# A Trainium2 attention and MLP kernel: a written-out program order in place of a planner, one pool of eight PSUM banks, and one head pair more on the half-array path

## The chip, the cores and the metric

The kernel runs on one core of one Trainium2 chip. The metric is the device time of one execution in microseconds (us), lower is better. Runs of the kernel before took 312.3, 311.33 and 309.93 us; the median is 311.33 us. Engines are named as in the profile: PE is the matrix engine, DVE the vector engine, ACT the scalar engine, POOL the general engine that here issues the loads, and SP the engine that issues the other DMAs.

## What is computed

Block-sparse attention over 4 batches of 8 heads, 768 positions and 64 dimensions, followed by an MLP over tokens and then over channels. Cut to what matters:

```python
scores = q @ k.T / sqrt(64)                        # per batch and head, 768 x 768
mask = window of +-1 block | first and last block row and column | 3 sampled blocks per block row
attn = softmax(where(mask, scores, -1e9))          # blocks are 32 x 32
x = (attn @ v), heads side by side                 # (4, 768, 512)
a1 = alpha1 * x + beta1
u = x + lam * (w_tok @ a1)                         # w_tok is 768 x 768
ch = relu((alpha2 * u + beta2) @ w_ch1) @ w_ch2    # 512 -> 2048 -> 512
out = u + lam * ch
```

## The kernel before

**Units of work.** The 32 heads are handled as 16 pairs (four pairs per batch). The transposed scores of a pair are cut into nine units of 1024 columns, each two PSUM banks, so there are 144 units. Per unit there is one exponential on ACT (PSUM to SBUF, f16) and the products with the values on PE. After the ninth unit the two accumulators are normalised on DVE (L701, L704) into `x_sb`.

**Two ways to make scores.** The first `NPE = 6` pairs (0 to 5) are *single* (`single`, L714): the scores of one head at a time, with a contraction of 88 rows. 64 of them are the head's dimensions and 24 are rows of the block mask, so the mask costs no separate step (matmuls L729, exponentials L744, values L769). Their transposed queries and keys come from transposes on PE (L641, helper L294) and copies out of PSUM (L363). The other ten pairs are *paired* (`paired`, L791): both heads of a pair are computed at once on two halves of the array, 64 rows each (`qk_group`, matmuls L850, in groups of two or three units). There is no room for mask rows there. After the exponential (L802) DVE takes the minimum with a tile `maskT` that holds zeros where the mask is off (L807). Their queries and keys are transposed by DMA transposes that SP issues (`xt`, L668 to L673), two for each pair, from a staging tile `rel` of which there are three.

**The mask tile.** DVE makes 24 rows (`mrow`, L550), SP writes them to DRAM (`mout`, L557), and SP reads them back in 18 transfers that spread each row over the partitions of `maskT` (`min_`, L561 to L572). The planner releases this step by `MASK_AT = 28`.

**The MLP.** Per batch: scale and shift on DVE (L942, L950), the token product on PE (L962, in groups of 18 matmuls), the residual add (L972), the second scale (L978), a transpose (by SP's DMA at L1010, or on PE at L1000). Then comes the channel MLP in half batches of 384 tokens: 16 first products (L1044, four matmuls each), each followed by a relu on ACT (L1057) or on DVE (L1061), then second products (L1106), a residual add on DVE (L1123) and a store that SP issues (L1130).

**Loads.** POOL issues them in a fixed order (`LOADS`, L43, then the later pairs). From pair 8 on (p > NPE + 1) each waits for a flag that DVE writes (L417), which POOL reads with a one-element copy (L397).

**What sets the order.** The kernel's source holds a planner. Every step is a `Job` (L340) with an engine, a cost, a priority and its dependencies; an event loop (L1233 to L1363) plays the engines against time and issues the job with the lowest priority key that can go. It also decides by simulated free times which bank a step takes and, for steps that can run on either, whether ACT or DVE does them. Where PE would be idle in the plan, `fill` (L254) issues matmuls on zeros (L252). `pin_order` (L67) then fixes the instruction order of each engine, and `bank_order` (L84) orders the users of each bank.

**PSUM.** Six banks are in one tile `ps6`, a seventh is `ps7`, and an eighth carries the tag `ops`. Score units take pairs of banks (b0+b1, b2+b3, b4+b5); single pairs take only the last two of these (`PAIRS[1:]`, L752).

Of the kernel before, what the change touches and what calls it, by code (L numbers as in the profile page):

```python
# [11 lines left out]
FP = mybir.dt.float32  # L12
# [20 lines left out]
NPAIR = H // 2  # L33
VW = D + 2
UN = 1024
NU = 9
NS = NPAIR * NU
NPE = 6
NET = 11
LEADS = (18, 18, 18, 18, 18, 18, 18, 18, 19, 18, 18, 18, 18, 18, 18, 18)  # L40
PATS = (800.0, 800.0, 800.0, 800.0, 1200.0, 800.0, 0.0, 800.0, 800.0, 400.0, 800.0, 800.0, 800.0, 800.0, 800.0, 800.0)
NUDGE = {}
LOADS = (  # L43
    "v 0", "q 1", "k 1", "v 1", "q 2", "k 2", "tok 0", "tok 1", "tok 2", "v 2", "lam", "a1",
    "b1", "q 3", "v 3", "k 3", "a2", "be2", "q 4", "k 4", "v 4", "w1 0", "w1 1", "w1 2",
    "w1 3", "q 5", "k 5", "v 5", "q 6", "k 6", "v 6",
)
PR = 1
EARLY = ('b0', 'b1')
OLD = True  # L50
MROW = (2, 3, 9)
W2AT = (0, 1, 2, 7.5)
NSPLIT = 0
UTN = 0
TOKP = 1
COVER = 800.0
NLD = 6
HOLD = 2
T0 = 6600.0
MASK_AT = 28  # L60
AHEAD = 13000.0
SCALE = 1.0 / 8.0
EXPB = -0.35667494
F16MAX = 65504.0

# [71 lines left out]
def kernel(  # L137
# [78 lines left out]
    ps6 = ps.tile([P, 6 * 512], FP, name="ps6", tag="ps6", bufs=1)  # L216
    ps7 = ps.tile([P, 512], FP, name="ps7", tag="ps7", bufs=1)
    ps6_name = [ps6[:].tensor.name]
    BANKS = tuple(f"b{i}" for i in range(6))
    ALL = BANKS + ("b6",)  # L220
    PAIRS = ("b0+b1", "b2+b3", "b4+b5")

    def bank(name, shape, dt=FP):
        t = ps7[:, :] if name == "b6" else ps6[:, ts(ALL.index(name), 512)]
        if dt != FP:
            t = t.bitcast(dt)
        t = t[:, 0 : int(np.prod(shape[1:]))]
        return t if len(shape) == 2 else t.rearrange("p (o c) -> p o c", o=shape[1])

    def two_banks(names):  # L230
        return ps6[:, ts(PAIRS.index(names), UN)]

# [17 lines left out]
    def keep_warm(n, w, name="b6"):  # L250
        for _ in range(n):
            nc.tensor.matmul(bank(name, [P, w]), warm[:, 0:P], warm[:, 0:w], start=True, stop=True)  # L252

    def fill(ns):  # L254
        free = [x for x in ("b6", "b0", "b1") if slots[x] > 0]
        while ns > 60.0 and free:
            w = min(512, int(ns * 2.4))
            keep_warm(1, w, free[0])
            ns -= w / 2.4 + 3.0

    keep_warm(7, 512)
    keep_warm(2, P)
# [17 lines left out]
    rel0 = wk.tile([P, 2, NT, 2 * D], BF, name="rel", tag="rel", bufs=3)  # L280

    def first_cast(a):
        for i, src in enumerate((q2f, k2f)):
            sl = src[:, a, :].rearrange("p (o d) -> p o d", o=NT)
            dst = rel0[:, a, :, i * D : (i + 1) * D]
            if a == 0 and i == 1:
                nc.scalar.copy(out=dst, in_=sl)
            else:
                nc.vector.tensor_copy(out=dst, in_=sl)

    def transposes(rel, a, name, slots=range(NT)):
        tps = bank(name, [P, NT, P], BF)
        for o in slots:
            nc.tensor.transpose(tps[:, o, :], rel[:, a, o, :], identb[:])  # L294
        return tps.rearrange("p o c -> p (o c)")
# [3 lines left out]
    flatA = transposes(rel0, 0, "b0", range(0, 3))  # L299
    flatB = transposes(rel0, 0, "b1", range(3, 6))  # L300
    bqs = []
    for w in range(2):
        t = ps.tile([P, 512], FP, name="ops", tag="ops", bufs=1) if w else bank("b2", [P, 512])
# [15 lines left out]
    keep_warm(7, P)  # L319
    for j in range(2, NQB):  # L320
# [4 lines left out]

    ACT_COPY = dict(ACT=790.0)
    dma_free = [8000.0]
    SEM = 70.0  # L330
    DRAIN = 166.0
    free_at = dict(NEVER=1e9, NONE=0.0, PE=T0, ACT=T0, DVE=T0, POOL=4800.0, SP=T0)
    slots = dict(
        **{b: 1 for b in ALL}, ops=1, eT=NET, head=NQB, vext=NV, ld=NLD, rel=3,
        x=NXB, uT=3, hts=2, a1p=2, ub=2, ot=2, w2b=1,
    )
    jobs = []
    now = [0.0]

    class Job:  # L340
        def __init__(self, eng, dur, prio, fn, deps=(), take=(), give=(), lat=None):
            self.eng = eng if isinstance(eng, tuple) else (eng,)
            self.dur, self.prio, self.fn = dur, prio, fn
            self.deps = list(deps)
            self.take, self.give = take, give
            self.lat = lat
            self.alt = {}
            self.xfer = None
            self.late = 0.0
            self.moves = False  # L350
            self.done = None
            self.gate = None
            self.marks = []
            self.n = len(jobs)
            if prio in NUDGE:
                self.prio = (prio[0] + NUDGE[prio],) + prio[1:]
            jobs.append(self)

    def copy(eng, out, in_):
        if eng == "ACT":  # L360
# [4 lines left out]
    def Copy(prio, fn, deps, take=(), give=(), only=False):  # L365
        j = Job(("DVE", "NEVER") if only else ("ACT", "DVE"), 550.0, prio, fn, deps, take, give)
        j.alt = ACT_COPY
        return j

    def pieces(u):  # L370
        f = u * 512
        while f < (u + 1) * 512:
            jt, c = divmod(f, S)
            w = min(S - c, (u + 1) * 512 - f)
            yield f - u * 512, jt, c, w
            f += w

    def mmt(n, cols):
        return n * (max(cols, 60) / 2.4 + 2.7)

    def dve(n, rate, base):
        return base + n / 0.96 / rate

    pairs = [(b, n) for b in range(B) for n in range(NPAIR)]
    tl = {}
# [3 lines left out]
    def Load(xfer, prio, fn, deps=(), take=()):  # L389
        j = Job("POOL", 720.0, prio, fn, deps, take)  # L390
        j.xfer = xfer
        return j

    def load(name, src_ap, shape, dt, tag, bufs, xfer, prio, deps=(), take=(), held=None):
        def fn():
            if held is not None:
                nc.gpsimd.tensor_copy(out=held_[0:1, held : held + 1], in_=flag[0:1, held : held + 1])  # L397
            t = wk.tile(shape, dt, name=name, tag=tag, bufs=bufs)
            nc.gpsimd.dma_start(t[:], src_ap)  # L399
            return t  # L400

        return Load(xfer, prio, fn, deps, take)

    ld = {}
    wload = {}
    w2tile = []
    wtk_tile = []

    after = []
    flag = pp.tile([P, 3 * len(pairs)], BF, name="flag", tag="flag")  # L410
    held_ = pp.tile([P, 3 * len(pairs)], BF, name="held", tag="held")

    def raise_flag(p, i):
        c = 3 * p + i

        def fn():
            nc.vector.memset(flag[0:1, c : c + 1], 0.0)  # L417

        j = Job("DVE", 70.0, (0, p), fn)
        after.append((j, (p - 2) * NU + HOLD + 3 * i))  # L420
        return [j]

    def load_pair(p, prio, which="qkv"):
        for i, (src, dt, nm) in enumerate(((q, BF, "q2"), (k, BF, "k2"), (v, F16, "v2"))):
            if p == 0 and nm != "v2" or nm[0] not in which:
                continue
            hold_ = p > NPE + 1
            ld[p, nm] = load(
                nm, pair_ap(src, *pairs[p]), [P, 2, NT * D], dt, "ld", NLD,
                1300.0 if p < 2 else 980.0, prio, raise_flag(p, i) if hold_ else [], take=("ld",),  # L430
                held=3 * p + i if hold_ else None,
            )
            ld[p, nm].late = 1500.0 if hold_ else 0.0

    def plain(eng, dur, prio, fn, deps=(), **kw):
        return Job(eng, dur, prio, fn, deps, **kw)

    def load_wtk(g, prio):
        def fn():
            if g == 0:  # L440
                wtk_tile.append(wk.tile([P, NT, S], BF, name="wtk", tag="w2b", bufs=1))
            nc.gpsimd.dma_start(
                wtk_tile[0][:, 2 * g : 2 * g + 2, :],
                moe_w_tok.rearrange("(p o) s -> p o s", o=NT)[:, 2 * g : 2 * g + 2, :],
            )

        wload["tok", g] = Load(2100.0, prio, fn, take=("w2b",) if g == 0 else ())

    def load_bc(t, src, prio):
        def fn():  # L450
            nc.gpsimd.dma_start(t[:], src.unsqueeze(0).to_broadcast([P, DM]))

        return Load(720.0, prio, fn)

    def load_be2(prio):
        def fn():
            with nc.allow_non_contiguous_dma(reason="512 elements"):
                nc.gpsimd.dma_start(be2T[:], moe_beta2.rearrange("(o p) -> p o", p=P))

        return Load(200.0, prio, fn)  # L460

    def load_w1(g, prio):
        def fn():
            nc.gpsimd.dma_start(w1b[:, g, :], moe_w_ch1[ts(g, P), :])
# [931 lines left out]
```

## Time and profile before

| what | before |
|---|---|
| runs | 312.3, 311.33, 309.93 us |
| the profiled execution's span | 307.7 us |
| PE matmuls busy, share | 298.9 us, 97% |
| DVE busy, share | 207.5 us, 67% |
| ACT busy, share | 205.8 us, 67% |
| POOL busy, share | 52.6 us, 17% |
| bytes moved by DMA | 30.81 MB, 47174 packets |
| exponentials of single pairs | 55 instructions (the first unit in two parts), 52.2 us |
| exponentials and minimums of paired units | 90 each, 86.9 us and 60.4 us |
| relus on ACT and on DVE | 104 and 24 |
| half-array score matmuls (L850) | 240 |
| single-pair score matmuls (L729) | 144 |

The page comes from one execution, whose own time is the span of 307.7 us. The medians are of whole runs and lie a few us above a span. Matmul records overlap, since a record is a matmul's latency and the next begins before it ends: the busy share of PE tells that it always has something in hand, not that it streams at full rate. Rates are read from how far apart the starts of equal matmuls are. Rows with "SPq" are the DMA instructions of SP: their times are those of issuing, and the transfer lands later. Times in a row of the timeline are start and length in us.

### The profile page before, as it was taken

What the parts mean: (1) busy time and instruction counts of PE and PEld (TensorE: products, weight loads), DVE (VectorE), ACT (ScalarE), POOL (GpSimd) and SP (SyncE); (2) the same over time, 40 slices, a digit from 0 to 9 for tenths busy, and PEclk for the clock granted to TensorE, in tenths of its full rate; (3) what the DMA queues carried; (4) which work ended last, traced back from release to release, by engine and by line L of the source; (5) the groups of instructions that cost most, each with busy time, mean ns of one, the idle gap of its engine ahead of it and who ended that gap; (6) DMA issues with size and microseconds to landing.
All of it is one profiled execution on the core that took longest, in us unless ns stands there. A gap on an engine that the chain in (4) does not pass through costs nothing.

```text
span 307.7 us, 7558 instructions
## 1 busy us (share of the span) xinstructions
PE 298.9 (97%) x3161; PEld 188.1 (61%) x3194; DVE 207.5 (67%) x435; ACT 205.8 (67%) x270; POOL 52.6 (17%) x91
## 2 busy tenths in 40 slices
PE   7999999998999999999999999999999999999995
PEld 3677788674655765565656665565756656555444
DVE  4688998987889986757988696888868730010111
ACT  5999987987787567756765857766858728428000
POOL 4747323001132121211221111120000000000000
PEclk9999999999999999999999999999999999999999
DMA  5999999996453768295275834465020120010121
GB/s 147 186 253 221 213 204 210 172 125 109 69 89 66 132 71 144 51 110 110 49 134 87 128 62 111 87 87 77 3 63 34 28 29 33 34 70 0 54 84 68
DMA packets 47174, 30.81 MB, mean 100 GB/s; under 512 B 27516, under 2 KB 43044, under 8 KB 47140
## 3 DMA queue, kind: packets, MB, share of 16 engines
q0 software_dynamic: 15984, 15.47, 32.5%
q1 hardware_dynamic: 30940, 14.61, 22.7%
q8 instruction: 25, 0.41, 0.5%
q10 hardware_dynamic: 216, 0.24, 0.2%
q14 instruction: 9, 0.07, 0.1%
HBM read 32.04 MB, written 6.33 MB: 125 GB/s over the span
## 4 chain that ended last, share of the span: by engine, by line
PE 89%; DMA 6%; POOL 2%; issue 1%; ACT 1%; DVE 0%
PE ps L1044 26%; PE ps L1106 21%; PE ps L962 10%; PE ops L883 8%; PE ps L850 7%; PE ps L729 5%; PE ops L1106 5%; PE ops L769 3%; DMA wtk<-in_moe_w_tok_dram 3%; DMA kx<-rel 3%; DMA q2f<-in_q_dram 1%; PE ps L506 1%; PE ps L294 1%; PE ps L252 1%; POOL v L399 0%
## 5 line engine op out<-in xcount | busy, mean ns | idle before, releaser
L802 ACT ACTIVATE eT<-ps 128x1024 f16<-128x1024 f32 x90 | 86.9, 1023 | 32.6 <-PE ps L850 28.6
L1044 PE MATMUL ps<-uT,w1b 128*128 128x384 bf16 (+1 forms) x512 | 93.1, 326 | 0.1
L1057 ACT ACTIVATE hts<-ps,b1t 128x384 bf16<-128x384 f32 x104 | 59.9, 581 | 37.9 <-PE ps L1044 32.2
L1106 PE MATMUL ps<-w2b,hts 128*128 128x512 bf16 (+1 forms) x293 | 72.4, 373 | 1.5 <-issue 0.2
L807 DVE TENSOR_TENSOR eT<-eT,maskT 128x1024 f16<-128x1024 f16 x90 | 60.4, 687 | 17.6 <-ACT eT L802 17.5
L1044 PEld LDWEIGHTS <-w1b 128*128 128x128 bf16 x512 | 46.3, 98 | 29.0 <-ACT eT L802 1.2
L1106 PEld LDWEIGHTS <-hts 128*128 128x128 bf16 x400 | 36.6, 98 | 36.1 <-issue 2.2
L744 ACT ACTIVATE eT<-ps 128x1024 f16<-128x1024 f32 (+1 forms) x55 | 52.2, 1019 | 4.8 <-PE ps L729 4.5
L883 PEld LDWEIGHTS <-eT 128*128 128x128 f16 x720 | 30.8, 97 | 15.1 <-issue 4.0
L962 PE MATMUL ps<-a1p,wtokT 128*128 128x128 bf16 x576 | 36.6, 219 | 0.0
L883 PE MATMUL ops<-vext,eT 128*128 128x65 f16 x720 | 36.0, 193 | 0.0
L962 PEld LDWEIGHTS <-wtokT 128*128 128x128 bf16 x576 | 33.3, 98 | 2.9 <-issue 0.5
L1123 DVE TENSOR_TENSOR ot<-x_sb,ps 128x512 f32<-128x512 f32 (+1 forms) x20 | 13.4, 672 | 28.3 <-PE ps L1106 28.3
L729 PE MATMUL ps<-qx,kx 88*128 88x512 bf16 (+1 forms) x144 | 31.4, 326 | 0.6 <-ACT kx L318 0.6
L397 POOL COPY held<-flag 1x1 bf16<-1x1 bf16 x24 | 9.4, 393 | 122.5 <-DVE flag L417 122.5
L850 PE MATMUL ps<-qx,kx 64*128 64x512 bf16 (+1 forms) x240 | 25.6, 326 | 1.2 <-DMA kx<-rel 1.2
L769 PEld LDWEIGHTS <-eT 128*128 128x128 f16 x432 | 18.3, 97 | 5.0 <-DVE x_sb L704 0.6
L769 PE MATMUL ops<-vext,eT 128*128 128x65 f16 x432 | 20.2, 193 | 0.1
L972 DVE TENSOR_TENSOR x_sb<-x_sb,ps 128x384 f32<-128x384 f32 x32 | 17.5, 550 | 3.9 <-PE ps L962 3.5
L704 DVE TENSOR_TENSOR x_sb<-ops,rcp 128x384 f32<-128x384 f32 x32 | 17.8, 558 | 1.1
L1123 DVE TENSOR_TENSOR ot<-x_sb,ops 128x512 f32<-128x512 f32 (+1 forms) x5 | 3.2, 634 | 22.5 <-PE ops L1106 22.5
L850 PEld LDWEIGHTS <-kx 64*128 64x128 bf16 x240 | 8.9, 94 | 14.7 <-issue 4.4
(68 smaller groups left out, 229.5 us busy)
## 6 DMA issues: line engine op xcount, KB each, us to landing
out_dram<-ot SPq DMA_DIRECT2D x23, 256.0 KB
v<-in_v_dram POOLq DMA_DIRECT2D x16, 192.0 KB, 5.3
q<-in_q_dram POOLq DMA_DIRECT2D x15, 192.0 KB, 3.8
k<-in_k_dram POOLq DMA_DIRECT2D x15, 192.0 KB, 4.8
w1b<-in_moe_w_ch_dram POOLq DMA_DIRECT2D x4, 512.0 KB, 9.9
w2b<-in_moe_w_ch_dram POOLq DMA_DIRECT2D x4, 512.0 KB, 14.7
wtk<-in_moe_w_tok_dram POOLq DMA_DIRECT2D x3, 384.0 KB, 9.6
maskT<-mask_rows SPq DMA_DIRECT2D x14, 72.0 KB
```

Of the source, the lines that this page charges most:

```text
L704: nc.vector.tensor_tensor(out=x_sb[:, s0 : s0 + NT, h * D : (h + 1) * D], in0=op[:, :, 0:D], in1=rcp[:].unsqueeze(2).broadcast_to([P, NT, D]),
L729: nc.tensor.matmul(sps[:, f - u * UN : f - u * UN + w], kx[h][0:KC, ts(jt, P)], qx[h][0:KC, c : c + w], start=True, stop=True,)
L744: nc.scalar.activation(eT[:, c], sps[:, c], AF.Exp, bias=EXPB, scale=SCALE)
L769: nc.tensor.matmul(ops[p, a][:, t * VW : t * VW + D + 1], eTs[p, u][:, ts(i - u * GU, P)], vx[:, a, jt, 0 : D + 1], start=(i % HT == 0), s ...
L802: nc.scalar.activation(eT[:], sps[:], AF.Exp, bias=EXPB, scale=SCALE)
L807: nc.vector.tensor_tensor(out=e, in0=e, in1=maskT[:, u, :].unsqueeze(1).broadcast_to([P, 2, 512]), op=ALU.min,)
L850: nc.tensor.matmul(sps[:, a * 512 + lo : a * 512 + lo + w], kx[sl][r, ts(jt, P)], qx[sl][r, c : c + w], start=True, stop=True,)
L883: nc.tensor.matmul(ops[p, a][:, t * VW : t * VW + D + 1], eTs[p, u][:, a * 512 + c * P : a * 512 + (c + 1) * P], vx[:, a, jt, 0 : D + 1], ...
L962: nc.tensor.matmul(tp[:, j, :], wtokT[:, s, ts(3 * g + j, P)], tl["a1p", p][:, s, :], start=(s == 0), stop=(s == NT - 1),)
L1044: nc.tensor.matmul(hp[:, 0:nc_], w1b[:, dk, ts(f, P)], uTs[b][:, dk, hf * HS : hf * HS + nc_], start=(dk == 0), stop=(dk == 3),)
L1057: nc.scalar.activation(hts[kk][:, f, :], hp[:, 0:HS], AF.Relu, bias=b1t[:, f : f + 1], scale=1.0)
L1106: nc.tensor.matmul(cps[kk, mi][:, 0:w], hts[kk][:, nk, ts(m, P)], w2tile[0][:, nk, lo : lo + w], start=(nk == 0), stop=(nk == 15),)
```

## The change

The planner, its jobs, priorities and tuning constants go. In their place stands a string `ORDER` of 1460 words, and a function for each kind of word; a loop calls them in the string's order, so the string sets the order on every engine's queue. A word is a kind, a number and, after a colon, a bank or an engine. `q46:2` is the score unit 46 in the bank pair 2, `e46` its exponential, `m46` its minimum with the mask, `p`/`r` its value products for the two heads, `n` a normalisation. `f15:1` is the first channel product 15 in bank 1, `g15:a` its relu on ACT (`:d` on DVE), `h` four matmuls of a second product, `o` and `s` its residual add and store. `tq5` and `tk5` are the DMA transposes of pair 5's queries and keys, `cq5` and `ck5` the casts ahead of them. `M0`, `N0` and `O0` to `O17` are the mask's rows, their write and the 18 spreading transfers; `l...` are loads, `F` flags, `z` a zero matmul.

What changes in the work and its place:

- `NPE` goes from 6 to 5: pair 5 becomes a paired one. Head transposes on PE go from 72 matmuls to 60, single-pair score matmuls from 144 to 120, half-array score matmuls from 240 (35 groups) to 264 (36 groups), minimums on DVE from 90 to 99, DMA transposes of queries and keys from 20 to 22.
- All eight banks are one tile; a score unit may take any of the pairs 0+1, 2+3, 4+5, 6+7, in the single phase too.
- Relus on DVE go from 24 to 51, on ACT from 104 to 77.
- Zero matmuls go from 36 to 17; after the first score unit only one is left (`z309:7`).
- Loads wait for a flag from pair 7 on (27 loads, before 24).
- `M0` and `N0`, the mask's rows and their write, stand near the start of the order. On SP the order is then tq5, O0, tk5, O1 to O16, tq6, O17, tk6, tq8, tk7, tq7, and so on. Before, it was the write, the 18 transfers, and then the transposes of pairs 6 and 7.
- On DVE the first minimum, `m45`, stands ahead of the relu `g13:d`; on PE `f15:1` uses the bank that `g13` frees.

The core of the diff:

```diff
-NPE = 6
+NPE = 5
-LEADS = (18, 18, 18, 18, 18, 18, 18, 18, 19, 18, 18, 18, 18, 18, 18, 18)
-MASK_AT = 28
-AHEAD = 13000.0
+HELD = NPE + 2
+
+ORDER = """
+lv0 lq1 lk1 cq0 q0:1 lv1 q3:2 e0 M0 q1:3 hm0 lq2 H1:1 N0 e3 q2:1 lk2 hq1:d hk1:d lt0 e1 F24 cv0 q4:0
+lt1 q7:2 e2 p0:6 lt2 p1 cq1 e4 F30 z309:7 q5:1 lv2 p2 p3 e5 lc0 q6:0 ck1 p4 H2:7 lc1 e6 n0 q8:1 lc2
...
+p31 k3:4 x2 e33 n6 q38:0 x3 q37:3 e38 cq5 k4:3 ah6 tq5 e37 lx2 ck5 q36:0 u2 r31:4 r32 hq9:a O0 u3
+q39:3 x4 r33 e36 r34 tk5 r35 U1:2 n7 e39 U0:5 q44:0 O1 ah7 k5:3 v0:a bh7 O2 e44 F25 cq6 q40:3 bh6
...
+O10 f3:3 L2 f4:0 O11 n9 g3:a f1:7 a4 g4:a O12 f2:2 g1:a b4 O13 f6:6 g2:a O14 q46:2 g6:d q47:0 e46
+q45:1 f7:7 O15 S1 e47 k8:6 F21 F40 lq7 cv5 O16 g7:d e45 lq8 f0:4 tq6 S3 f5:1 x8 g0:a F39 S2 O17
+q50:3 g5:a q48:1 q49:2 S0 k9:0 e48 tk6 F33 S5 e49 f11:1 S4 f9:2 x9 e50 g11:d f17:5 g9:a u9 f8:0 m45
+g17:a f13:1 g8:a q53:3 g13:d q52:2 q51:1 e52 h0:0 ck7 m50 lq9 e51 f15:1 cq7 F45 ck9 lk8 f14:5 F47 S6
...
+h121 s29 o28 h122 h123 s28 h124:3 h125 o30 h126 h127 s30 o31 s31
+"""
...
+    psum = ps.tile([P, 8 * 512], FP, name="psum", tag="psum", bufs=1)
...
+    @on("O")
+    def _(i):
+        c, o, e, f = spread[i]
+        dst = maskT[:].rearrange("p u c -> p (u c)").rearrange("p (o w) -> p o w", o=NT)
+        src = mask_dr.rearrange("(m f) w -> m f w", f=3)
+        nc.sync.dma_start(
+            dst[c:P:16, o:e, :], src[:, f, :].unsqueeze(1).broadcast_to([8, e - o, S])
+        )
...
+    @on("q")
+    def _(n, j):
+        p, u = divmod(n, NU)
+        sps[n] = t = psum[:, ts(j, UN)]
+        if p < NPE:
+            for a, jt, c, w, f in cut(u * UN, (u + 1) * UN):
...
+    for word in ORDER.split():
+        kind = word[: next(j for j, c in enumerate(word) if c.isdigit())]
+        n, _, arg = word[len(kind) :].partition(":")
+        args = (int(arg) if arg.isdigit() else arg,) if arg else ()
+        step[kind](int(n), *args)
+
+    bank_order(tc, list(nc.cur_bb.bb.instructions), psum[:].tensor.name, 8)
```

## The prediction, as put on record before the run

> **What bounds the kernel now.** I read the page first (busy shares, granted clock, DMA row), then the chain that ended last, busy time by stretch, the groups by form, and SyncE's timeline.
>
> ```profile
> span 307.7 us, 7558 instructions
> PE 298.9 (97%) x3161; PEld 188.1 (61%) x3194; DVE 207.5 (67%) x435; ACT 205.8 (67%) x270; POOL 52.6 (17%) x91
> PEclk9999999999999999999999999999999999999999
> DMA  5999999996453768295275834465020120010121
> ```
>
> PE is the bound, at full granted clock; the DMA engines are full from about 8 to 61 us. The chain of waits is 89% PE; its long pieces give PE's rates, and its one long transfer after the start is a transpose:
>
> ```profile
> 63.46 7.79 DMA kx<-rel
> 180.96 2.01 PE ps L962 x36
> 253.99 10.40 PE ps L1044 x64
> 269.57 3.45 PE ops L1106 x16
> ```
>
> So 128 columns stream in 0.056 us, 384 in 0.163, 512 in 0.216. The transfer feeds the first scores of pair 6, the first pair that runs two heads on two halves of the array:
>
> ```profile
> 71.30 0.61 PE L850 MATMUL ps<-qx,kx 64*128 64x512 bf16 x6 [1.20 <-DMA kx<-rel]
> ```
>
> Those 1.20 us are the only DMA wait of PE after start-up. By stretch (busy us of each engine, granted clock, DMA share, GB/s):
>
> ```profile
> core 0: us, PE busy (x) PEld busy (x) DVE busy (x) ACT busy (x) POOL busy (x), PEclk, DMA share, GB/s
> 20.00:30.00 10.00, 9.95 (x148) 7.40 (x145) 9.68 (x19) 9.97 (x12) 6.92 (x12) 1.00 1.23 252
> 50.00:60.00 10.00, 9.95 (x143) 7.73 (x141) 9.11 (x23) 8.62 (x12) 2.88 (x4) 1.00 1.27 191
> 60.00:70.00 10.00, 9.95 (x123) 6.85 (x120) 9.01 (x22) 9.09 (x11) 0.00 (x0) 1.00 1.00 123
> ```
>
> The eye must not stop at PE: until 30 us ScalarE is full too (exponentials of the single pairs), VectorE is at 90% to 70 us, and DMA is saturated to 60 (packets overlap, hence shares over 1). PE looks full at 20 to 30 us because zero matmuls of L252 fill its waits. SyncE's queue holds the matter that decides:
>
> ```profile
> 40.84 0.31 SPq L557 DMA_DIRECT2D mask_rows<-maskT  x1
> 45.17 16.39 SPq L569 DMA_DIRECT2D maskT<-mask_rows  x18
> 62.01 1.32 SPq L670 DMA_TRANSPOSE qx<-rel  x1
> 63.46 2.54 SPq L670 DMA_TRANSPOSE kx<-rel  x1
> 73.25 0.69 DVE L807 TENSOR_TENSOR eT<-eT,maskT 128x1024 f16<-128x1024 f16 x1
> ```
>
> The 18 mask transfers go ahead of the first transposes, and the mask's first use is 12 us after the last issue: the mask costs nothing.
>
> **Time base.** The sum is made against this execution. First score matmul at 6.65 us, last matmul begins at 303.9, tail 3.8. The median of the runs, 311.33, is 3.6 above the span; I add that.
>
> **PE's work.** Between 6.65 and 303.9 lie 297.3 us, aligned record by record with the program: 282.9 of streaming, 3.9 of zero matmuls (L252), 8.0 of switching into and out of half-array mode (35 groups, 0.115 each way), 1.2 the wait above, 1.2 small waits at start. The change:
> - Pair 5's scores move to half-array pieces: a single pair's 12 pieces of 512 and 12 of 256 columns take 12 x (0.216 + 0.109) = 3.90; two at a time, 1.95. Saves 1.95.
> - Its 12 head transposes leave PE: 12 x 0.056 = 0.67.
> - Groups of half-array scores become 36: +0.23.
> - Zero matmuls after the start fall to one (0.13): 3.8 of occupancy removed, which is a gain only if real work stands ready.
>
> No-wait end of PE: 6.65 + 280.4 + 8.3 = 295.4, against 303.9. The most to be gained is 8.5 us. Whatever lag L PE has in the new order is paid out of this: time = 295.4 + L + 3.8 + 3.6 = 302.8 + L.
>
> **Start-up lag.** Exponentials start every 0.92 us (group L744) and 45 of them are still single: 45 x 0.92 = 41.4, so they end near 48 us whatever PE does (before, the 45th ended at 59.1 in another order). Summing row costs along the new order, PE reaches the score group that needs an earlier exponential at least 2.2 us before that is done. Before lost 5.2 here (3.9 + 1.2). Ends 2.2 and 5.2; I take 3, nearer the new order's own sum.
>
> ```profile
> L744 ACT ACTIVATE eT<-ps 128x1024 f16<-128x1024 f32 x53 | 51.3, 1035 | 4.3 <-PE ps L729 4.0
> L807 DVE TENSOR_TENSOR eT<-eT,maskT 128x1024 f16<-128x1024 f16 x90 | 60.4, 687 | 17.6 <-ACT eT L802 17.5
> L1057 ACT ACTIVATE hts<-ps,b1t 128x384 bf16<-128x384 f32 x104 | 59.9, 581 | 37.9 <-PE ps L1044 32.2 <-DVE hts L1061 1.7
> L1061 DVE TENSOR_SCALAR hts<-ps,b1t 128x384 bf16<-128x384 f32 x24 | 14.8, 616 | 2.9 <-PE ps L1044 1.5 <-ACT hts L1057 0.7
> ```
>
> **VectorE.** Pair 5 needs mask minimums: 9 at a start-to-start 0.60 = 5.4. 27 relus move from ScalarE: +27 x 0.533 = 14.4 here, -27 x 0.479 = 12.9 there. Between the first minimum and the second channel matmul's main part (65 to 107 us) VectorE has 39.3 us of work in 41.6 of PE's: little room to catch up. Ends 0 and 2; I take 0.5.
>
> **The mask's queue, the deciding step.** The row write (N0) now goes at about 8 us, so the 3.9 us for which SyncE waited on it go. But pair 5 needs its scores early, so SyncE's order becomes: q transpose of pair 5, mask transfer 0, k transpose of pair 5, transfers 1 to 16, q transpose of pair 6, transfer 17, k transpose of pair 6, then pairs 8 and 7. Three transposes that stood behind the mask now stand ahead of its last transfer, in a queue that shares engines with saturated loads. The first can issue at about 42.3 (pair 5's q landed at 41.45, then the cast). The first packets of mask transfer 0 came 3.8 us after issue, so the queue moves from 46.1. The 18 mask transfers took 17.3 us against loads (packets from 49.0 to 66.3). A transpose alone has 768 packets at 1056 per us: 0.8 us. Against loads it goes packet for packet with them (at 79.0 to 80.4 us some 150 per us): 5.1 us. Loads' last chunk landed at 70.14, so two transposes meet them fully, the third hardly; and loads served beside them no longer slow the mask. I take 3.3, near the middle. Last mask transfer landed: 46.1 + 17.3 + 3T + 1 = 64.4 + 3T: 66.8, 79.7, and 74.3 at 3.3.
>
> Who waits: pair 5's first minimum stands in VectorE's order ahead of the relu that frees the bank of the next channel matmul; casts, load flags (so POOL's loads) and all later minimums queue behind it and shift with it. PE wants that bank at 65.4 in the no-wait sum and gets it 1.5 after the mask (minimum 0.65, relu 0.69, two hand-overs). L = 64.4 + 3T + 1.5 - 65.4 = 0.5 + 3T: 2.9, 15.8, and 10.4. It takes in the start-up lag and the wait for pair 5's k transpose.
> **The clock.** Before has no PE gap over 1.4 us, and no row with a lowered clock. Its first nine zero matmuls do show the slow rate:
>
> ```profile
> 1.19 3.21 PE L252 MATMUL ps<-warm 128*128 128x512 bf16 x9 [1.19 <-DVE warm L248]
> ```
>
> 3.21 us against 9 x 0.216 = 1.94: one cold start costs 1.3. A PE stall of 5 us or more could bring it again: ends 0 and 2.6 (two stalls), I take 1.3. The Trainium skill, "TensorE: Matmul & The Clock Gate", Part 1, "What's actually happening", speaks against the change here: after an idle window of about 3.4 us the array drops to half clock and needs as long a busy stretch to return. By it, an estimate, one stall costs about 1.7 us and the sum would be 0.4 higher; no run here shows a gap long enough.
>
> **Sum:** 302.8 + 10.4 + 0.5 + 1.3 = 315.0 us, 1.2% above 311.33.
>
> **Other edits.** One pool of eight banks, copies swapped between ScalarE and VectorE (a few of 0.5 to 0.7 us), three more held loads (POOL idle over 80%): at nothing, hidden under the exponentials to 48 us and PE afterwards; without that cover, 1 us in all.
>
> **Rivals.**
> 1. The mask lands in time and the change is faster. The load backlog doesn't oppose the queue (T = 0.8), L falls to the start-up's 3, no cold start: 305.8. For it: start-up runs ahead of before by some microseconds, and the queue starts 3 us sooner. Against it: DMA share 1.27 at 50 to 60 us. It decides when the last mask transfer lands before about 67 us; break-even is L = 8.5, T = 2.7, landing at 72.4.
> 2. Within 1%: T of 1.6 to 3.1, landing at 69 to 73.7; gain of PE's work and the new wait cancel: about 311. For it: work in the queues is conserved, and before finished the same packets by 71.
> 3. All three transposes meet full loads (T = 5.1): 302.8 + 15.8 + 1.8 = 320.4. Against it: loads are done by 70.
> 4. VectorE becomes the bound without a late mask: 305.8 + 2 = 307.8.
>
> That the change doesn't do what it says is excluded: by count, half-array pieces go from 240 to 264, head transposes from 72 to 60.
>
> **How the numbers follow.** About 1% is what a measurement of this kernel can tell from no change. T from 0.8 to 5.1 weighed evenly, with the 1.8 of clock and VectorE where L is long: below 308.2 needs T under 1.6, with rival 4 some 0.27; 308.2 to 314.4, T to 3.1, 0.25; above, 0.48 (my case 0.33, rival 3 0.15). Range 304.5 to 320.5 from the ends of T; the likeliest case alone spans 313 to 317.5.
>
> **What would show it.** After: VectorE idle 5 to 11 us before its first minimum, released by maskT; PE stalled at the channel matmul from about 66 to 76 with a dip in granted clock; a wait of 1 to 3 us at the first half-array scores (about 58); the single exponentials done by 48. Wrong if that minimum starts within 2 us of its exponential.

## The result, and the profile after

The changed kernel took 327.65 us (325.08 to 330.8, 4 runs), against 311.81 us for the kernel before beside it: a ratio of 1.0488, with a 95% interval from 1.0429 to 1.0546. Medians are of all runs of a kernel, while a ratio leaves out those over 1.5% above its fastest run, so a ratio can be a little below the quotient of the medians. The forecast was 315.0, with a range up to 320.5. The sign was right. The size was wrong by 12.7 us, and the time lies outside the range.

The same first lines of the page, for the profiled execution of the changed kernel:

```profile
span 326.5 us, 7476 instructions
PE 300.9 (92%) x3140; PEld 187.7 (58%) x3163; DVE 224.6 (69%) x469; ACT 187.8 (58%) x244; POOL 52.4 (16%) x94
PEclk9769999979996999999999999999999999999999
DMA  6997999998696596995515003340000303210022
```

PE's share falls from 97% to 92%, and the clock row, flat before, has dips in three places: the second and third slices (8 to 24 us), the ninth (65 to 73) and the thirteenth (98 to 106). Busy us by stretch, with granted clock, DMA share and GB/s:

```profile
core 0: us, PE busy (x) PEld busy (x) DVE busy (x) ACT busy (x) POOL busy (x), PEclk, DMA share, GB/s
10.00:20.00 10.00, 4.16 (x40) 2.83 (x41) 2.64 (x9) 2.44 (x3) 3.84 (x7) 0.59 1.16 204
60.00:70.00 10.00, 7.47 (x115) 5.53 (x115) 7.46 (x21) 5.46 (x12) 2.11 (x6) 0.99 1.17 187
90.00:100.00 10.00, 5.08 (x88) 3.34 (x86) 4.98 (x11) 4.37 (x6) 1.90 (x4) 0.85 1.58 144
```

In the first and last of these stretches every engine is idle for about half of the time or more while DMA is full. The long pieces of the chain that ended last are four transfers, here with start and length:

```profile
7.45 6.55 DMA qx<-qx
...
53.72 15.74 DMA kx<-rel
...
78.17 4.07 DMA maskT<-mask_rows
...
90.85 10.06 DMA qx<-rel
```

And the list of waits says who stood behind each (total, times, longest):

```profile
DVE maskT L491 <- DMA qx<-qx: 6.6, 1, 6.6
DVE rel L527 <- DMA qx<-rel: 6.0, 1, 6.0
PE psum L605 <- DMA qx<-rel: 5.9, 1, 5.9
DVE eT L620 <- DMA maskT<-mask_rows: 3.4, 1, 3.4
PE psum L605 <- DMA kx<-rel: 2.4, 1, 2.4
```

The last two waits are in the queue that the prediction watched: the mask, and the keys of pair 5. The second and third are for a transpose of pair 7. The first begins at 7 us, where the prediction looked for nothing.

**A ledger of PE.** I aligned PE's records with the program and took, by stretch, the time between two starts less the streaming in between, less 0.115 us for each switch of array mode, less the zero matmuls. What is left, called PE's loss below, is its waiting and its slow clock. The streaming work after 6.5 us is 280.2 us, by the changed kernel's own matmuls at the rates of the kernel before (predicted 280.4). The program has 72 switches (8.3), and the last matmul begins at 322.4. So the lag L, which the prediction put at 10.4 plus 1.8, measures 27.4:

| stretch, us | before: waits, fillers in brackets | after | what waits in after |
|---|---|---|---|
| first score to 20 | 0.6 (1.8) | 9.2 | DVE for qx<-qx, then slow clock |
| 20 to 60 | 0.7 (2.2) | 2.9 | exponentials |
| 60 to 70 | 1.4 | 3.0 | kx<-rel of pair 5 |
| 70 to 90 | 0.1 | 3.4 | the mask, slow clock |
| 90 to 110 | 0.0 | 7.5 | qx<-rel of pair 7, slow clock |
| 110 to the end | -0.3 | 1.3 | |

### The profile page after: what moved, and what is told of

Its sections match the earlier page's. It is cut to its first block, busy times and chain, and to the rows that moved or that the text cites. A ratio compares the mean times of both kernels' runs of the same rounds, so it can differ in the third digit from the quotient of the medians.

```text
span 326.5 us, 7476 instructions
## 1 busy us (share of the span) xinstructions
PE 300.9 (92%) x3140; PEld 187.7 (58%) x3163; DVE 224.6 (69%) x469; ACT 187.8 (58%) x244; POOL 52.4 (16%) x94
## 4 chain that ended last, share of the span: by engine, by line
PE 64%; DMA 16%; DVE 10%; ACT 4%; issue 3%; SPq 1%; ACTq 0%; DVEq 0%
PE psum L768 21%; PE psum L802 19%; PE psum L629 7%; PE psum L714 6%; PE psum L605 6%; DMA kx<-rel 5%; DVE eT L620 4%; PE psum L595 3%; DMA qx<-rel 3%; ACT eT L615 3%; DMA qx<-qx 2%; DMA v<-in_v_dram 2%; DMA uT<-ub 1%; DMA maskT<-mask_rows 1%; DMA eqt<-tabs_c 1%
## 5 line engine op out<-in xcount | busy, mean ns | idle before, releaser
L615 ACT ACTIVATE eT<-psum 128x1024 f16<-128x1024 f32 (+1 forms) x145 | 138.9, 1019 | 57.1 <-PE psum L605 35.7
L768 PE MATMUL psum<-uT,w1b 128*128 128x384 bf16 (+1 forms) x512 | 94.5, 330 | 3.0 <-DVE hts L784 1.9
L802 PE MATMUL psum<-w2b,hts 128*128 128x512 bf16 (+1 forms) x377 | 87.1, 370 | 1.2
L782 ACT ACTIVATE hts<-psum,b1t 128x384 bf16<-128x384 f32 x77 | 44.0, 582 | 50.3 <-PE psum L768 48.8
L629 PEld LDWEIGHTS <-eT 128*128 128x128 f16 x1152 | 45.4, 98 | 13.9 <-issue 3.6
L629 PE MATMUL psum<-vext,eT 128*128 128x65 f16 x1152 | 49.2, 195 | 0.2 <-ACT eT L615 0.2
L784 DVE TENSOR_SCALAR hts<-psum,b1t 128x384 bf16<-128x384 f32 x51 | 30.4, 611 | 14.6 <-PE psum L768 14.2
L714 PE MATMUL psum<-a1p,wtokT 128*128 128x128 bf16 x576 | 37.5, 221 | 0.0
L605 PE MATMUL psum<-qx,kx 64*128 64x256 bf16 (+1 forms) x264 | 28.9, 335 | 8.3 <-DMA qx<-rel 5.9
L595 PE MATMUL psum<-qx,kx 88*128 88x512 bf16 (+1 forms) x120 | 26.9, 343 | 7.5 <-DVE flag L419 6.9
L723 DVE TENSOR_TENSOR x_sb<-x_sb,psum 128x384 f32<-128x384 f32 x32 | 17.4, 547 | 3.0 <-PE psum L714 3.0
L663 DVE TENSOR_TENSOR x_sb<-psum,rcp 128x384 f32<-128x384 f32 x32 | 17.8, 557 | 1.1
L595 PEld LDWEIGHTS <-kx 88*128 88x128 bf16 x120 | 9.9, 101 | 12.7 <-DVE flag L419 7.4
```

What stands on the lines that cost most here:

```text
L595: nc.tensor.matmul(t[:, f : f + w], kx[h][0:KC, ts(jt, P)], qx[h][0:KC, c : c + w], start=True, stop=True,)
L605: nc.tensor.matmul(t[:, a * 512 + f : a * 512 + f + w], kx[h][r, ts(jt, P)], qx[h][r, c : c + w], start=True, stop=True,)
L615: nc.scalar.activation(eTs[n][:, c], t[:, c], AF.Exp, bias=EXPB, scale=SCALE)
L629: nc.tensor.matmul(ops[p, a][:, t * VW : t * VW + D + 1], eTs[n][:, c : c + P], vext[p % NV][:, a, jt, 0 : D + 1], start=(jt == t == 0), s ...
L663: nc.vector.tensor_tensor(out=x_sb[:, s0 : s0 + NT, h * D : (h + 1) * D], in0=t[:, :, 0:D], in1=rcp[:].unsqueeze(2).broadcast_to([P, NT, D ...
L714: nc.tensor.matmul(t[:, j, :], wtokT[:, s, ts(3 * g + j, P)], a1p[p][:, s, :], start=(s == 0), stop=(s == NT - 1),)
```

## The experiments

Times are medians; ratios are to the kernel before on the same chip, and the time of the kernel before was 311.51 us beside e1 to e4, 312.73 beside e5 to e8 and 311.49 beside e9 to e12. What one edit is worth is therefore read from the difference of two ratios, times 311.5 us; by the intervals such a difference is known to some 3 us. In e1 to e4 the line numbers in the profile are 5 to 7 lower than those of the changed kernel, since the string is broken into fewer lines.

### e1: the rows' step alone

```diff
-... e0 M0 q1:3 hm0 lq2 H1:1 N0 e3 ...
+... e0 q1:3 hm0 lq2 H1:1 e3 ...
-... F31 hk3:d q9:3 ...
+... F31 hk3:d M0 N0 q9:3 ...
```

> The words M0 and N0 (the mask's rows on DVE and their write) move from the start of the order to behind hk3:d, some 10 us later; nothing else changes. Theory A: M0 stands in DVE's queue and waits until 14.0 us for the copy qx<-qx, with the head copies, and by them the loads, queued behind it; this shift of 7 to 9 us runs through the whole start and moves the transposes of pair 5 and the mask with it. Then this kernel is 7 to 9 us faster than the changed one, 319 to 321 us, and the last mask transfer lands near 74 us where it landed at 82.2. Rival B: the DMA queue sets the end whatever PE does before, the mask lands at 80 or later as now, and less than 3 us are gained (325 or more).

Measured: 321.2 us (318.53 to 322.74), ratio 1.0305 [1.0227, 1.0383]. Theory A holds in the main, at the lower end of what it expected: by the ratios 5.7 us of the 15.2 (6.4 by the medians) were one DVE instruction in the wrong place, where 7 to 9 had been expected. PE's loss up to 60 us falls from 12.1 to 5.0. What that instruction did is seen in DVE's timeline of the changed kernel:

```profile
6.81 0.64 DVE L330 CAST rel<-k2f 128x384 bf16<-128x384 f32 x1
14.03 0.35 DVE L491 TENSOR_SCALAR maskT<-qx 24x768 f16<-24x768 bf16 x1 [6.58 <-DMA qx<-qx]
14.30 0.34 DVE L558 COPY qx<-qx 24x768 bf16<-24x768 bf16 x1
14.66 0.55 DVE L386 COPY qx<-psum 64x768 bf16<-64x768 bf16 x1
```

The word M0 reads mask rows that a DMA copies from one `qx` tile to another. That DMA is issued at 7.45, behind the other start-up DMAs, and lands at 14.0. DVE stands still for it, and behind DVE stand the copies of head 1 that PE's next scores need (PE idle 6.89 us), the casts that free the load buffers, and so POOL: the load of pair 5's queries is issued at 36.35 us (before: 28.79) and lands at 48.54 (before: 41.45). In the kernel before the same instruction stood at 40 us and waited for nothing:

```profile
40.46 0.35 DVE L551 TENSOR_SCALAR maskT<-qx 24x768 f16<-24x768 bf16 x1
```

The late mask was not moved out of the way by this: the last mask transfer lands about 5 us sooner, at 76.8 (changed kernel: 82.2; expected: near 74), but PE's lead over it has grown, and DVE now waits longer:

```profile
DVE eT L614 <- DMA maskT<-mask_rows: 6.9, 1, 6.9
```

### e2: the clock of the start alone

```diff
-... cv0 q4:0
+... cv0 z512:0 (28 times) q4:0
```

> 28 zero matmuls of 512 columns (6.0 us at full rate) are put ahead of score unit 4, in PE's idle time of 8 to 15 us; the wait of DVE stays. Theory C: the lowered clock after the idle time is a cost of its own, about 1.3 us for one cold start (the price that the prediction took); then 326 us, and the granted clock at 10 to 20 us goes from 0.59 to above 0.9. Rival: the clock costs nothing here, since ScalarE sets the pace at the start, and the time stays at 327.5; or it costs 3 us or more, 324.5 or less.

Measured: 324.6 us, ratio 1.0442 [1.0370, 1.0515], against 1.0488 [1.0429, 1.0546] without: the intervals overlap. The granted clock at 10 to 20 us does go from 0.59 to 1.00:

```profile
10.00:20.00 10.00, 9.17 (x87) 5.03 (x85) 3.82 (x13) 4.26 (x6) 3.72 (x7) 1.00 1.16 205
```

PE's loss up to 60 us, fillers counted as loss, falls from 12.1 to 9.3. By 90 us it is 18.4 and 18.6: the late mask takes the gain back. So the clock's price at the start is some 3 us of PE's time in these two profiles. Of the whole time it is 3 us by the medians and 1.4 by the ratios, and the intervals allow none; the runs don't settle how much.

### e3 and e4: the mask's transfers early, with the rows late and early

```diff
-... hk5:d p12 ...
+... hk5:d O0 O1 O2 (and so on to) O17 p12 ...
```

> As e1_rows_late, and the 18 mask transfers move ahead of the transposes of pairs 5 and 6, to behind hk5:d (about 24 us). Theory A with the mask as the second cause, and the wait of 90 to 101 us as its consequence (casts and load flags queue on DVE behind the first minimum, and the loads that come late meet the transposes of pair 7): 306 to 310 us, faster than before. Rival: the wait at 90 to 101 us comes from the order of its own transposes, those of pair 8 ahead of those of pair 7, and stays: 312 to 316 us. Rival: the mask among the early loads delays them as much as it is freed later: 318 or more.

> The 18 mask transfers alone move to behind hk5:d; the rows stay early, so the start keeps its wait of 6.6 us. Theory: the start's loss stays (some 10 to 12 us of PE), the losses after 60 us, some 15 us, go: 313 to 317 us if the wait at 90 to 101 us goes with the mask, 319 to 322 if it stays. Rival B (the queue's work is the same wherever the mask stands): less than 3 us faster than the changed kernel, 325 or more.

Measured: e3 324.26 us (ratio 1.0393 [1.0336, 1.0450]), e4 326.75 (1.0449 [1.0358, 1.0541]). e3 is about 3 us slower than e1, with intervals that overlap, and e4 equals the changed kernel within its interval: the mask early gives nothing. Of e3's rivals the last is right in its time, and the one before it in its wait, which stays, though not in its time. e4 comes to the 325 or more of its rival. Put at 20 to 38 us, the 18 transfers take the time of the loads of pairs 3 and 4: in e3 PE loses 8.0 us between 30 and 50 (e1: 0.9), pair 4's key load lands at 37.5 us (before: 29.6), and the exponentials starve:

```profile
20.00:30.00 10.00, 8.67 (x137) 6.74 (x134) 7.40 (x16) 9.91 (x11) 4.56 (x7) 1.00 1.23 240
30.00:40.00 10.00, 5.36 (x76) 3.96 (x76) 5.17 (x13) 4.89 (x5) 3.36 (x6) 1.00 1.15 214
40.00:50.00 10.00, 9.54 (x105) 7.59 (x106) 7.80 (x17) 5.55 (x6) 2.74 (x4) 0.66 1.00 184
```

The wait for the mask is gone in both (PE's loss at 80 to 90 us is -0.0 and -0.1), and yet the wait at 90 to 101 us stays at 6.1 and 6.7 us. That one is no consequence of the mask.

### e5: pair 7's transposes first

```diff
 e1, and
-... ck7 ... cq7 ... tq8 ... tk7 ... tq7 ...
+... ck7 tk7 ... cq7 tq7 ... tq8 ...
```

> As e1_rows_late (321.2 us), and the two transposes of pair 7 move up to directly behind their casts, ahead of those of pair 8, which PE needs later. Theory D: the wait of PE at 90 to 101 us (5.3 us in e1) comes from the order of these transposes beside a burst of seven loads: it goes, and 316 to 317.5 us are left. Rival: the burst of loads itself, or the late cast of pair 7's keys, sets it wherever the transpose stands: 320 or more.

Measured: 317.65 us, ratio 1.0176 [1.0110, 1.0243]. Theory D holds in the main: 3.5 us by the medians and 4.0 by the ratios, though the two intervals touch, and PE's loss at 90 to 101 us falls from 5.3 to 1.8. In the changed kernel the three transposes went out in the order 8, 7, 7, beside seven loads at 84 to 92 us that had waited for DVE to empty their buffers:

```profile
87.94 1.21 SPq L564 DMA_TRANSPOSE qx<-rel  x1
89.20 1.61 SPq L564 DMA_TRANSPOSE kx<-rel  x1
90.85 1.63 SPq L564 DMA_TRANSPOSE qx<-rel  x1
```

The queries of pair 7, for which PE waited, were last and took 10.1 us. The 1.8 us that stay in e5 have another cause, on the side of the rival: DVE's queue stands for a load of the same burst, and PE's token product behind it waits. From the chain of e5:

```profile
81.60 9.93 DMA k<-in_k_dram
```

### e6: the mask ahead of pair 5, as it was ahead of pair 6

```diff
-... e0 M0 ... N0 e3 ... (O0 to O17 spread from tq5 to tk6)
+... e38 M0 N0 O0 (and so on to) O17 cq5 k4:3 ah6 tq5 ...
```

> The mask's rows, their write and all 18 transfers stand directly ahead of the casts and transposes of pair 5, at about 42 us, as they stood ahead of the first pair's transposes in the kernel before. Theory E: pair 5 wants the mask and its transposes about 12 us sooner than pair 6 did, and the full DMA queues can't give both in any order: the mask lands near 66 and no longer stalls VectorE, but PE waits 8 to 12 us at the first half-array scores for kx<-rel, and the time is 319 to 323, no better than e1. Rival: it was the order alone, the three transposes ahead of the mask; then the wait at the scores stays under 4 us and 313 to 316 us result.

Measured: 330.27 us, ratio 1.0584 [1.0527, 1.0640]: worse than theory E expected (319 to 323), with the wait that it named. The mask no longer stalls DVE, and PE waits instead where the expectation put it, for 15.6 us, not 8 to 12:

```profile
65.28 1.33 SPq L564 DMA_TRANSPOSE qx<-rel  x1
66.71 3.03 SPq L564 DMA_TRANSPOSE kx<-rel  x1
```
```profile
75.31 1.46 PE L605 MATMUL psum<-qx,kx 64*128 64x256 bf16 x8 [15.56 <-DMA kx<-rel]
```

### e7 and e8: six single pairs in the written-out order

```diff
-NPE = 5
+NPE = 6
-HELD = NPE + 2
+HELD = NPE + 1
-... tq5 ... tk5 ... m45 (to) m53 ... r45:6 ... r49 ...
+... r42 H10:1 hq10:d hk10:a ... f3:3 H11:1 hq11:d hk11:a ... r45 ... r49:6 ...
```

e7 is this with e1's late rows; e8 has e5's edit as well.

> As e1_rows_late, but six single pairs again in the written-out order: pair 5 gets its scores with mask rows, 12 head transposes and four copies, and loses its nine minimums and two DMA transposes. PE's work grows by 2.4 us. Theory E: the losses of PE at 60 to 80 us (8.3 us in e1) fall to about 1; net 5 us faster than e1, 315 to 317 us. Rival: the losses there have another cause (a VectorE that is too full, the loads) and stay: 321 to 324.

> e5 and e7 together: six single pairs, late rows, pair 7's transposes first. If the three causes are apart and add up, 309 to 312 us, the time of the kernel before. If they share one wait, 315 or more.

Measured: e7 326.39 us (1.0443 [1.0371, 1.0515]), e8 319.79 (1.0248 [1.0184, 1.0313]): both theories missed, for a reason that they left out (e8 lies in the 315 or more of its alternative, but not by a shared wait). With tq5 gone nothing holds SP, and 17 mask transfers go out at once after the rows:

```profile
15.04 0.30 SPq L498 DMA_DIRECT2D mask_rows<-maskT  x1
19.83 17.39 SPq L514 DMA_DIRECT2D maskT<-mask_rows  x17
```

So e7 repeats e3's fault (PE's loss at 30 to 50 us: 6.7). It does show no wait for the mask at 60 to 90 us (1.4 in all; e1: 9.3).

### e9: six single pairs, the mask at its old time

```diff
 e8, with the rows' words moved
+... e38 M0 N0 cq5 k4:3 ah6 ...
```

> As e8 (six single pairs, pair 7's transposes first), but the mask's rows and their write stand at about 40 us, directly ahead of cq5, so that the 18 mask transfers go out from about 44 us as in the kernel before; in e7 and e8 they went out at once from about 18 us and took the loads of pairs 3 and 4 with them. Theory E (a first half-array pair at 57 us is too soon for mask and transposes, one at 72 us is not): PE's losses are 3 to 4 us up to 60 us, none at the mask, some 3 after; 302.8 + 2.6 + 7 = 312.4, the range 310 to 314, the time of the kernel before. Rival: VectorE, with 27 more relus, is the bound in the new order whatever the mask does: 316 or more.

Measured: 310.07 us (10 runs), ratio 0.9950 [0.9912, 0.9988]: the time of the kernel before, or 0.5% less. Theory E holds in the time and at the mask. This is the changed kernel's order, its one pool of banks and its 51 relus on DVE, with pair 5 single, the rows at 45 us and pair 7's transposes first. PE's loss is 8.7 us over the whole span, of which 0.4 lie between 60 and 80 and 6.7 up to 60, where 3 to 4 were expected (see e10 for the start):

```profile
span 309.7 us, 7510 instructions
PE 302.5 (98%) x3175; PEld 189.0 (61%) x3175; DVE 220.1 (71%) x462; ACT 189.1 (61%) x246; POOL 53.1 (17%) x94
```
```profile
45.38 0.30 SPq L498 DMA_DIRECT2D mask_rows<-maskT  x1
49.65 14.18 SPq L514 DMA_DIRECT2D maskT<-mask_rows  x17
64.13 1.32 SPq L564 DMA_TRANSPOSE qx<-rel  x1
65.50 0.62 SPq L514 DMA_DIRECT2D maskT<-mask_rows  x1
66.24 8.81 SPq L564 DMA_TRANSPOSE kx<-rel  x2
```

DVE is busier than before (71% against 67%) and no bound; the rival falls.

### e10: the clock at the mask's wait alone

```diff
 e5, and
-... e51 f15:1 ...
+... e51 z512:4 (18 times) f15:1 ...
```

> As e5_pair7_first (317.65 us), with 18 zero matmuls of 512 columns (3.9 us) ahead of the channel product that waits for the mask, at 72 to 76 us; the wait stays. Theory C: the granted clock of 0.60 after this wait costs 2 us (12 matmuls of the channel product took 3.91 us in e5 where 1.96 is their rate): 315 to 316.5 us, and the clock at 76 to 82 us near 1. Rival: VectorE has the backlog anyway, a slow PE there costs nothing: 317 or more.

Measured: 319.27 us (316.86 to 322.62), ratio 1.0291 [1.0208, 1.0373], against e5's 1.0176 [1.0110, 1.0243]: not faster, with intervals that overlap. The clock did what was meant. First e5, then e10:

```profile
76.00:82.00 6.00, 4.89 (x18) 2.37 (x19) 5.96 (x17) 2.77 (x7) 4.38 (x9) 0.60 0.60 82
```
```profile
76.00:82.00 6.00, 6.00 (x32) 2.65 (x29) 4.60 (x14) 1.98 (x3) 2.66 (x6) 1.00 0.45 57
```

The 12 matmuls of the channel product after the wait took 2.12 us where e5 took 3.91 (e5's row, then e10's):

```profile
77.11 3.91 PE L768 MATMUL psum<-uT,w1b 128*128 128x385 bf16 x12 [5.11 <-DVE hts L784]
81.10 2.12 PE L768 MATMUL psum<-uT,w1b 128*128 128x385 bf16 x12
```

The time didn't follow. But the profiled execution of e10 lost 5.5 us before 20 us where e5 lost 1.9, with nothing changed there. The trace says why: at the start the array first ran at half rate, and it went to full rate at 17.4 us in e10 and at 5.7 in e5. The first eight score matmuls, for one, took 2.77 us in e10 and 1.51 in e5. In e1 the full rate came at 10.4 us, in e9 at 13.8, in the other profiles of the changed order at 4.3 to 5.8. The granted clock of the profile shows 1.00 there all the same. So single profiles of this start differ by some 3.5 us. From 60 to 110 us e10 lost 7.7 us, the zero matmuls counted, and e5 11.4; but a PE that comes later also finds more of the mask landed (DVE waited 3.0 us for it, in e5 6.6), and the clock's price at this wait stays open.

### e11: the kernel before without its fillers

```diff
-        while ns > 60.0 and free:
+        while False and free:
```

> The kernel before with its filler matmuls between real work taken out (20 of the 36 zero matmuls; those ahead of the first head stay), all else the same. The prediction's step: the filler only occupies time in which nothing else stands ready, so its removal changes nothing, 311 to 312.5 us. Rival: without filler the clock drops in the idle time of 6 to 30 us, and the kernel before becomes 2 to 4 us slower.

Measured: 311.36 us (10 runs), ratio 1.0007 [0.9971, 1.0043]. The prediction's step holds: the fillers between real work take nothing and give nothing, within 0.4%. The profile of e11 comes to the full rate of the array late, at 13.9 us (kernel before: 4.1), as e9 and e10 do; one profile of each can't tell whether the fillers have to do with it.

### e12: pair 6's query transpose behind the mask

```diff
 e5, and
-... f0:4 tq6 S3 ... S2 O17
+... f0:4 S3 ... S2 O17 tq6
```

> As e5_pair7_first, and the query transpose of pair 6 moves from ahead of the last mask transfer to behind it. Theory: a transpose ahead of the mask costs 3.3 us of its landing (the prediction's T); at 70 us, with most loads landed, between 1 and 3: the mask wait of VectorE (6.6 us in e5) falls to 4 or 5, 315 to 316.5 us. Rival: the last transfer is set by its own issue, since at most eight of the queue are under way, and not by the transpose: 317 or more.

Measured: 316.1 us, ratio 1.0161 [1.0102, 1.0219]. DVE's wait for the mask is 4.8 us (e5: 6.6), as the theory has it. The gain of time is 1.5 us by the medians and 0.5 by the ratios, within the intervals, so that it is not shown:

```profile
DVE eT L620 <- DMA maskT<-mask_rows: 4.8, 1, 4.8
```

It is the lowest median of an order with five single pairs here, 6 us above e9.

## Why the prediction was wrong, point by point

- **PE's work: right.** The changed kernel's matmuls come to 280.2 us of streaming where 280.4 were worked out, and in stretches without a wait the loss is 0.0 (e1 at 100 to 110 us), so the rates hold. The gain of PE's work was real, and was spent on waits.
- **The row write at about 8 us, "so the 3.9 us for which SyncE waited on it go": the step that failed.** I priced the word N0, which SP issues, and not M0, the DVE instruction ahead of it, whose input comes by a DMA that lands at 14.0. SP no longer waited for the write, but now stood until 51.5 us for pair 5's cast; and DVE, with the whole start queued behind it, stood 6.6 us. Moved alone (e1) the step is worth 5.7 us of time by the ratios (6.4 by the medians) and 7.1 us of PE by 60 us. The start-up lag of 3 that the prediction took was 12.1 by 60 us with it, and 5.0 without (3.6 in e5).
- **The mask's queue, L = 0.5 + 3T: the kind of wait was right; that its size came out is in part luck.** Without the start's wait, in e5, pair 5's first transpose is issued at 43.4 us, where I put 42.3, and the last mask transfer lands at 75.5, where I put 74.3. By the prediction's own sum, 47.2 + 17.3 + 1 + 3T, T is 3.3, and in the changed kernel, 51.5 + 3.8 + 17.3 + 1 + 3T = 82.2, it is 2.9. But that T is what the sum leaves over. In the packet records pair 5's two transposes moved some 150 packets per us beside the loads, as the prediction had it, and took 5.9 and 6.3 us in e5 (6.1 and 6.5 in the changed kernel): each more than the 5.1 at the top of its range. The mask's transfers behind them in e5 needed some 11 us, not 17.3, up to the next transpose at 70.5. The two errors cancel. The lag by 90 us in e5 is 13.2, of which 2.7 are there by 40 us; 12.2 was forecast. In the changed kernel it is 18.6, since all of this begins 8 us late. e6 and e9 fit one cause behind it: the loads fill the DMA engines to some 70 us, and mask and transposes fit beside them for a pair whose scores begin at 78 us (e9), not for one that wants them at 59 (e6).
- **The signs that were named.** In the changed kernel VectorE stood 3.4 us for the mask, not 5 to 11, and PE 1.9 us at the channel matmul, at 82 to 84 us; the wait for the mask has the stated size where PE is less late: in e1 (6.9), e2 (6.3) and e5 (6.6). The wait at the first half-array scores is 2.4 us, as stated, but ends at 69.6. The single exponentials end at 62.7 us, and at 54.3 in e5, not at 48: the 41.4 us for 45 of them held no wait between them.
- **Pairs 8 and 7, named in SP's order and not priced: the second term left out.** After the mask's wait the prediction let "casts, load flags (so POOL's loads) and all later minimums queue behind it and shift with it". A shift was not all: the loads came in one burst of seven and met the transposes of pairs 8 and 7. The last in line, which PE needed first, took 10.1 us: 6.2 us of PE at 90 to 101 us. e3 and e4 show that it needs no late mask, e5 that the order makes most of it, 3.5 of the 5.3 us of e1.
- **The clock: the mechanism shown, the price not.** The mean granted clock of the stretch is 0.59 and 0.60 after waits of PE of 6.9 and 5.1 us, and zero matmuls hold it at 1.00 (e2, e10). I took 1.3 us in all. The Trainium skill, "TensorE: Matmul & The Clock Gate", Part 1, "What's actually happening", has the array at half clock after an idle window of about 3.4 us. The rows agree on the half clock: after e5's wait the matmuls of 385 columns start 0.32 us apart, where 0.163 is the rate. They don't agree on the window: the clock fell after idle times of 2.1 us (e10, 0.57 at 66 to 69 us) and 2.4 (changed kernel, 0.50 at 70 to 73), and not after 3.3 (e12, 1.00 at 75 to 78). What one drop costs the kernel lies by e2 between nothing and 3 us, and is not settled.
- **VectorE and the other edits: nothing seen.** 27 more relus on DVE, one pool of banks and the copies cost nothing that can be seen once the three waits are gone (e9, 0.9950). The nine minimums of pair 5 are not in e9, so their price is not tested alone.
- **The rivals.** None held the case. Rival 3 (320.4) comes nearest, from the wrong source: its T of 5.1 was passed by two of the transposes, but the sum's T stayed at 3.3.
- **Slips in the working.** The row of nine zero matmuls holds seven of 512 columns and two of 128, 1.62 us at the full rate, so by their starts the cold start cost 1.4 us, not 1.3. The page's DMA row is full to 69 us, not 61. The ends of T give 305.7 and 320.4, so the 304.5 does not follow from them, and T from 1.6 to 3.1 is 0.35 of its span, not 0.25. None of these moves the sum by more than 0.1 us.

By the ratios e1 takes away 5.7 us, e5 another 4.0, e12 another 0.5, which is not shown, and e9 another 6.6 with pair 5 single again and the mask at its old time. The medians are 327.65, 321.2, 317.65, 316.1 and 310.07.

## What to carry to other kernels

When a step is moved, follow it to the first instruction of its chain and ask of that one what it reads and when that lands: here a 0.35 us instruction, moved some 26 us earlier (from 40.5 us), cost some 6 us. Then ask the same of every transfer that the new order names, also those after the stall that you expect, since a stall bunches the loads behind it and the next transposes meet them. Where a saturated queue serves a consumer that comes too soon, moving the consumer may be what is left: none of the orders tried here for five single pairs came nearer than 1.6% (e12), and six single pairs with the mask at its old time did (e9).

## What the runs showed of the hardware that was not expected

A transpose that takes 0.8 us alone took 15.7 us from issue to landing against loads (53.7 to 69.5 us in the changed kernel). Of these, 6.5 us are its own packets, and for most of the rest it stood behind the packets of the transpose ahead of it (55.4 to 61.5 us). Another took 10.1 us against a burst of seven loads; the one in the chain of the kernel before took 7.8. The small copy of 24 mask rows, issued at 7.45 us, took 6.55 us in the start's traffic.

The time at which the array first goes to full rate differs between executions of nearly the same start, from 4.1 us in the kernel before to 17.4 in e10, and the granted clock of the profile doesn't show it: it is read from the starts of equal matmuls.
